# A new order for the products of an attention and MLP-mixer kernel: values in rows

## The chip, the cores and the metric

The kernel runs on one core of one Trainium2 chip. The metric is the device time of one execution in microseconds, as the median of several runs.

## What is computed

For each of 8 x 12 heads, with a sequence of 448 and a head size of 64: scores, a squared ReLU, values. The heads side by side are the 768 channels of an MLP-mixer block.

```python
scores = scale * np.matmul(q, k.transpose(0, 1, 3, 2))
attn = np.maximum(scores, 0.0) ** 2 / S
x = np.matmul(attn, v)                       # then heads side by side
h = np.maximum(xt @ w_tok1, 0.0) @ w_tok2    # xt: tokens and channels swapped
u = x + h.transpose(0, 2, 1)
h2 = np.maximum(u @ w_ch1, 0.0) @ w_ch2
return u + h2
```

Inputs and output are float32; the products run in bfloat16 with sums in float32.

## The kernel before

**Work and names.** The heads are taken four at a time: 24 sets, three to a batch. For set s the operations are, with their names in the program's table:

- `ldk`, `ldq`, `ldv`: loads, by the POOL queue. `T` (L391) transposes k and q on TensorE for sets 0 to 11, and `cp` copies the result to SBUF. From set 12 on, `ik`/`iq` lay k and q out beside each other (L270 or L272) and `xk`/`xq` transpose them by DMA on the SP queue.
- `S{s}.{c}` (L432), c = 0 to 6: the scores of 64 rows of keys for four heads, four matmuls, each on one quarter of the array (64 x 64), into two PSUM banks. `r{s}.{c}.{0,1}` (L264 on ScalarE, L266 on VectorE) are the two evictions with ReLU, one per bank, and `q{s}.{c}` (L439, VectorE) is the square. Ten buffers `sq` hold squares.
- `V{s}.{c}` (L456): the value product of that square, again four matmuls on quarters of the array. The seven of a set add up in the same two banks, and `xe` (L466, L468) evicts them after the seventh.
- `X` (L491) or, from set 8, `xd` (SP queue) transposes for the token mixing; `t1` (L500), `rt`, `t2` (L509), `u` (L513) are its two products, the ReLU and the sum.
- `C1.{b}.{e}` (L545): the first channel product of batch b, twelve blocks of six matmuls on the whole array, evicted by `c1e`. The last two batches take a form with fewer products, `Q` (L617). `P` (L710): the second channel product, seven products of six matmuls for a pair of token tiles, added up by `a`, `b`, `c` and `f` (L725, L727) on VectorE and stored by `st`. `ub` are DMA transposes that bring u to the tokens' layout.
- `fill` (L806): small products without use, which occupy TensorE where the table puts them.

**What sets the order.** Nothing is scheduled at build time: a table, `ORDER`, is a text of some 1950 words, and `Order.run` emits the operations in its order. Each engine executes its own in that order and waits by semaphores for what they need. A word is an operation's name; `:A` or `:D` behind it puts the operation on ScalarE or VectorE, digits name the PSUM banks it writes (eight in all), and `fill:2*7` is seven fill products into bank 2. An operation that writes a bank waits until the operation that read it last is done. The table was written by a search with a model of the engines.

So a score waits for its two banks, that is, for two evictions of an earlier operation; a value waits for its square; an eviction waits for its score and for the buffer `sq`.

Of the kernel before, what the change touches and what calls it, by code (L numbers as in the profile page):

```python
# [61 lines left out]
ldf.1 ldk0.1 ldf.0 ldk0.0 ldk1.1 ldq1.0 cast1.0:A cast1.1:D ldk1.0 ldq1.1 ident cast0.0:A cast0.1:D ldv0.0 T0.1:0  # L62
ldv0.1 T0.0:1 cp0.1:A ldk2.0 cp0.0:D ldq2.1 fill:2*7 S0.0:23 S0.5:45 S0.4:67 ldq2.0 r0.0.0:A r0.0.1:D S0.2:01
r0.5.0:A r0.5.1:D ldk2.1 S0.1:23 r0.2.1:A r0.2.0:D ldv1.1 S0.6:45 r0.1.1:A r0.1.0:D S0.3:10 r0.6.1:A ldv1.0 q0.0:D
r0.6.0:A fill:3*4 T1.0:32 ldq3.1 r0.3.1:A r0.3.0:D ldk3.0 cp1.1:A cp1.0:D ldk3.1 q0.1:D r0.4.1:A fill:5*19 S1.2:54
ldq3.0 S1.3:01 q0.2:D r0.4.0:A S1.4:32 r1.2.0:A ldv2.1 q0.3:D fill:7*3 V0.0:76 r1.2.1:A q0.4:D ldv2.0 r1.3.1:A
S1.0:54 q0.5:D ldk4.0 V0.1 r1.3.0:A V0.2 r1.0.1:D r1.0.0:A wt1.0 T2.0:10 q0.6:D r1.4.1:A V0.3 r1.4.0:A wt1.1 cp2.1:D
V0.4 S1.1:45 cp2.0:A q1.0:D ldk4.1 q1.2:D r1.1.0:A ldq4.0 fill:2*12 S2.1:23 S1.6:01 r1.1.1:A q1.3:D V0.5 ldq4.1
r1.6.1:A V0.6 r1.6.0:D S2.2:45 r2.1.0:A ldv3.0 q1.1:D S1.5:10 xe0.1:A q1.4:D ldv3.1 r1.5.0:A q1.6:D r1.5.1:A wt2
xe0.0:A r2.1.1:D r2.2.0:A q1.5:D ldk5.0 X0.0:2 r2.2.1:A S2.0:61 q2.1:D S2.3:07 xc0.0:A V1.0:34 ldk5.1 r2.0.1:D  # L70
r2.0.0:A V1.1 q2.2:D V1.2 r2.3.0:A ldq5.0 S2.5:52 r2.3.1:A X0.1:1 q2.0:D ldq5.1 T3.0:60 r2.5.0:A xc0.1:D V1.3
r2.5.1:A q2.3:D wc1.1 V1.4 cp3.1:A cp3.0:D S2.6:71 V1.5 r2.6.1:D V1.6 r2.6.0:A S2.4:52 V2.0:60 ldv4.1 q2.5:D xe1.1:A
V2.1 xe1.0:A r2.4.0:D S3.1:17 ldv4.0 r2.4.1:A r3.1.1:D fill:4*4 S3.0:43 ldk6.1 r3.1.0:A X1.1:5 r3.0.1:D V2.2
r3.0.0:A S3.4:27 xc1.1:D t1.0.0:1 r3.4.0:A q2.4:D t1.0.1:3 r3.4.1:A rt0.0:D S3.3:45 rt0.1:A q2.6:D V2.3 r3.3.1:A
V2.4 q3.0:D S3.2:27 r3.3.0:A T4.0:13 q3.1:D r3.2.1:A V2.5 S3.6:54 r3.2.0:A cp4.1:D r3.6.1:A cp4.0:D V3.0:72 V2.6
r3.6.0:A V3.1 q3.2:D ldv5.0 S3.5:34 xe2.1:A t1.1.1:1 r3.5.1:D r3.5.0:A ldq6.0 t2.0.1:5 q3.3:D rt1.1:A X1.0:0 ldv5.1
xe2.0:A V3.2 q3.4:D S4.4:43 xc1.0:A ldk6.0 V3.3 u0.1:D S4.0:16 r4.4.0:A V3.4 X2.0:0 q3.5:D r4.0.1:A X2.1:5 t1.1.0:4
r4.0.0:A xc2.0:D q3.6:D t2.0.0:6 r4.4.1:A ldq6.1 V3.5 rt1.0:A xc2.1:D S4.3:01 u0.0:D V3.6 wc1.0 S4.1:34 r4.3.1:A
t2.1.0:5 r4.3.0:D r4.1.1:A t1.2.0:6 ldq8.0 q4.0:D xe3.0:A t1.2.1:1 xe3.1:A rt2.0:D ldk7.1 t2.1.1:0 u1.0:D r4.1.0:A
t2.2.0:4 ldq8.1 rt2.1:A u1.1:D X3.0:7 ldk7.0 t2.2.1:6 u2.0:D xc3.0:A S4.6:23 q4.1:D ldq7.1 S4.2:51 T5.0:04 u2.1:D  # L80
r4.2.1:A t1.3.0:7 r4.2.0:A ldq9.0 cp5.1:D cp5.0:A r4.6.1:D ldq7.0 C1.0.6:1 q4.2:D rt3.0:A q4.3:D r4.6.0:A V4.0:65
c1e0.6:A S5.0:43 q4.4:D V4.1 S4.5:07 r5.0.1:A r5.0.0:D V4.2 S5.5:21 r4.5.1:A r4.5.0:D C1.0.10:3 r5.5.1:A q5.0:D
r5.5.0:A q4.5:D V4.3 c1e0.10:A S5.1:47 q4.6:D S5.3:01 r5.1.0:A C1.0.11:2 r5.1.1:D r5.3.1:A q5.5:D r5.3.0:A t2.3.0:3
q5.1:D c1e0.11:A C1.0.9:4 ldk8.0 q5.3:D ldv6.0 u3.0:D S5.4:71 c1e0.9:A S5.2:02 ldv6.1 r5.4.1:D C1.0.7:3 r5.4.0:A
r5.2.0:D r5.2.1:A q5.4:D T6.0:41 c1e0.7:A q5.2:D V4.4 V5.0:72 cp6.1:A cp6.0:D S5.6:03 V4.5 V5.1 r5.6.0:D V4.6
r5.6.1:A V5.2 S6.4:41 ldv7.1 xe4.1:D xe4.0:A V5.3 S6.5:03 r6.4.0:A q5.6:D ldk8.1 V5.4 S6.6:65 r6.5.1:A V5.5 r6.5.0:D
# [30 lines left out]
ub2.3 q11.3:D r11.2.1:A C1.2.6:6 r11.2.0:A xe10.1:D xe10.0:A q11.4:D C1.2.2:4 r12.1.0:A xd10 q11.2:D r12.1.1:A
q11.5:D c1e2.6:A P2.1:0 q12.1:D iq14:A st4.0 c1e2.2:D C1.2.0:5 st4.1 ik15:A ldq18.0 f11.1:D ub2.5 iq15:D ldv13.0
V11.0:17 c1e2.0:A S11.6:23 ldv13.1 V11.1 r11.6.0:A r11.6.1:D S12.0:64 st2.1 V11.2 ldk18.1 S12.5:05 r12.0.1:A
r12.0.0:D V11.3 S13.1:23 r12.5.0:A ldq18.1 V11.4 q11.6:D S12.4:46 r12.5.1:A V11.5 ldq16.1 q12.0:D C1.2.4:0 r12.4.1:A  # L120
# [716 lines left out]
```

## Time and profile before

| | |
|---|---|
| median of 3 runs | 351.79 us (350.87 to 352.61) |
| profiled execution | 351.28 us, span 349.5 us |
| instructions | 8983 |
| busy: TensorE / VectorE / ScalarE / GpSimd | 340.4 / 303.4 / 216.5 / 92.2 us |
| mean granted TensorE clock | 0.998 |

In the lines that follow, PE is TensorE, PEld its weight loads, DVE VectorE, ACT ScalarE, POOL GpSimd, and SP the queue of DMAs beside them. A row of a timeline has the start in us from the span's start, the length, the engine, the line, the operation, output and inputs, and how many instructions were merged into it; in brackets stands idle time ahead of it and who ended it. A row by stretches has the busy time of PE, PEld, DVE, ACT and POOL, the granted clock, the share of the DMA engines and GB/s. A matmul's end is modelled, so starts are the safer reading.

### The profile page before, as it was taken

The page shows a single profiled execution, that of the slowest core. Times are in us where ns is not written, and L with a number is a line of the kernel's source. Part 1 is how long each engine was busy: PE and PEld are TensorE (multiplying, and loading weights), DVE is VectorE, ACT ScalarE, POOL GpSimd, SP SyncE. Part 2 cuts the span into 40 slices and gives each one's busy share as a digit, 9 for nine tenths or more (in the row PEclk, how much of TensorE's full clock was granted, in tenths as well). Part 3 has the DMA queues.
Part 4 walks back from the last instruction along what each step waited for, and adds up shares of the span by engine and source line. Part 5 has one row for each costly group of instructions (what it writes and reads, how often), then busy time and mean ns, then how long its engine had stood idle before and what let it go on. Part 6 is the DMA issues. An engine that isn't in the chain of part 4 may idle for free.

```text
span 349.5 us, 8983 instructions
## 1 busy us (share of the span) xinstructions
PE 340.4 (97%) x3598; PEld 190.9 (55%) x3598; DVE 303.4 (87%) x581; ACT 216.5 (62%) x443; POOL 92.2 (26%) x157
## 2 busy tenths in 40 slices
PE   8979999999999999999999999999999999999994
PEld 4546645555555555555555555544556565555662
DVE  2999998889999899988598999899898987678973
ACT  4999887687939099783497927768664411562000
POOL 8884627321461804117304201110200000000000
PEclk9999999999999999999999999999999999999999
DMA  8999997999999999799999925897863524710245
GB/s 152 166 151 183 190 179 106 160 167 112 151 145 182 176 166 190 139 217 172 196 241 134 177 40 94 130 138 153 146 124 86 115 59 89 154 36 0 58 150 156
DMA packets 93434, 48.74 MB, mean 139 GB/s; under 512 B 65808, under 2 KB 90064, under 8 KB 93392
## 3 DMA queue, kind: packets, MB, share of 16 engines
q0 software_dynamic: 25904, 21.47, 44.3%
q1 hardware_dynamic: 67168, 26.30, 42.4%
q8 instruction: 28, 0.46, 0.6%
q10 hardware_dynamic: 320, 0.39, 0.3%
q14 instruction: 14, 0.11, 0.1%
HBM read 43.38 MB, written 11.01 MB: 156 GB/s over the span
## 4 chain that ended last, share of the span: by engine, by line
PE 93%; ACT 4%; DVE 1%; issue 1%; ACTq 0%; DVEq 0%
PE m_ps L710 28%; PE m_ps L545 24%; PE sc_ps L432 9%; PE acc_ps L456 9%; PE m_ps L617 7%; PE t_ps L500 6%; PE h_ps L509 5%; ACT sq L264 3%; PE warm_ps L335 1%; PE kqT_ps L391 1%; PE x_ps L491 1%; DVE sq L439 1%; ACT xT L466 0%; DVE sq L266 0%; ACT kqT L270 0%
## 5 line engine op out<-in xcount | busy, mean ns | idle before, releaser
L264 ACT ACTIVATE sq<-sc_ps 128x448 bf16<-128x448 f32 x222 | 107.9, 572 | 15.3 <-PE sc_ps L432 15.0
L439 DVE TENSOR_TENSOR sq<-sq 128x896 bf16<-128x896 bf16 x168 | 97.0, 614 | 0.0
L545 PE MATMUL m_ps<-uT_sb,wc 128*128 128x448 bf16 x432 | 90.9, 353 | 0.0
L266 DVE TENSOR_SCALAR sq<-sc_ps 128x448 bf16<-128x448 f32 x114 | 66.8, 616 | 12.3 <-PE sc_ps L432 12.2
L264 ACT ACTIVATE r_sb<-m_ps 128x448 bf16<-128x448 f32 (+2 forms) x96 | 42.0, 464 | 45.0 <-PE m_ps L545 43.2
L545 PEld LDWEIGHTS <-wc 128*128 128x128 bf16 x432 | 40.4, 98 | 40.7 <-issue 6.6
L432 PE MATMUL sc_ps<-kqT 64*64 64x448 bf16 x672 | 59.2, 354 | 0.6 <-DVE kqT L272 0.2
L286 POOL DMA_DIRECT2D v_raw<-in_v_dram x48 | 29.3, 620 | 104.7 <-PE acc_ps L456 89.1
L456 PE MATMUL acc_ps<-sq,v_raw 64*64 64x448 bf16 x672 | 56.3, 354 | 0.3
L710 PEld LDWEIGHTS <-r_sb 128*128 128x128 bf16 x336 | 32.5, 98 | 22.9 <-issue 1.3
L286 POOL DMA_DIRECT2D kq_raw<-in_k_dram x48 | 30.2, 640 | 34.3 <-ACT side L270 16.8
L725 DVE TENSOR_TENSOR out_sb<-m_ps,u_sb 128x384 f32<-128x384 f32 x56 | 30.8, 551 | 6.8 <-PE m_ps L710 6.8
L432 PEld LDWEIGHTS <-kqT 64*64 64x64 bf16 x672 | 24.3, 105 | 18.4 <-issue 9.6
L710 PEld LDWEIGHTS <-sums 128*128 128x128 bf16 x252 | 24.5, 98 | 17.0 <-issue 0.4
L286 POOL DMA_DIRECT2D kq_raw<-in_q_dram x46 | 28.4, 628 | 19.8 <-ACT side L270 14.3
L710 PE MATMUL m_ps<-wc_t,r_sb 128*128 128x384 bf16 x168 | 31.2, 326 | 0.0
L710 PE MATMUL m_ps<-wc,r_sb 128*128 128x384 bf16 x168 | 30.6, 326 | 0.0
L513 DVE TENSOR_TENSOR uT_sb<-h_ps,xT 128x448 bf16<-128x448 f32 x48 | 28.6, 613 | 2.2 <-PE h_ps L509 2.2
L710 PE MATMUL m_ps<-wc_t,sums 128*128 128x384 bf16 x168 | 30.1, 326 | 0.0
L456 PEld LDWEIGHTS <-v_raw 64*64 64x64 bf16 x672 | 20.6, 106 | 16.4 <-issue 9.6
L727 DVE TENSOR_TENSOR out_sb<-m_ps,out_sb 128x384 f32<-128x384 f32 x42 | 22.9, 552 | 7.4 <-PE m_ps L710 7.2
L500 PE MATMUL t_ps<-x_sb,wt 128*128 128x256 bf16 (+1 forms) x216 | 25.0, 261 | 0.0
(65 smaller groups left out, 325.2 us busy)
## 6 DMA issues: line engine op xcount, KB each, us to landing
out_dram<-out_sb SPq DMA_DIRECT2D x52, 192.0 KB, 3.1
kq_raw<-in_k_dram POOLq DMA_DIRECT2D x48, 112.0 KB, 5.0
v_raw<-in_v_dram POOLq DMA_DIRECT2D x48, 112.0 KB, 4.6
kq_raw<-in_q_dram POOLq DMA_DIRECT2D x46, 112.0 KB, 5.0
wc<-in_moe_w_ch_dram POOLq DMA_DIRECT2D x2, 1152.0 KB, 10.7
wc<-in_moe_w_ch_dram POOLq DMA_DIRECT2D x3, 576.0 KB, 9.2
u_sb<-uT_sb SPq DMA_TRANSPOSE x54, 3.4
sums<-in_moe_w_ch_dram POOLq DMA_DIRECT2D x1, 576.0 KB, 10.8
```

The source lines that it names most:

```text
L264: nc.scalar.activation(out, ps, AF.Relu)
L266: nc.vector.tensor_scalar(out=out, in0=ps, scalar1=0.0, scalar2=None, op0=ALU.max)
L286: nc.gpsimd.dma_start(out=raws[t][s % NR[t]][64 * half:64 * (half + 1)], in_=src[b, h0:h0 + 2].rearrange('e (p c) d -> p e (c d)', c=KC))
L432: nc.tensor.matmul(o.ps[e][64 * half:64 * (half + 1), :S], lhsT=lhsT, rhs=rhs, start=True, stop=True, skip_group_check=True)
L439: sq_ops[s, c] = [add(Op(f'q{s}.{c}', 'DVE', lambda o: nc.vector.tensor_tensor(out=buf, in0=buf, in1=buf, op=ALU.mult), ev))]
L456: nc.tensor.matmul(o.ps[half][64 * e:64 * (e + 1), :S], lhsT=r[rows, e, c * D:(c + 1) * D], rhs=sq[rows, e, :], start=c == 0, stop=c == KC ...
L500: nc.tensor.matmul(o.ps[:, j, :], lhsT=wt1[:, c, j * 128:(j + 1) * 128], rhs=x_sb[:, p0:p1, c, :], start=c == 0, stop=c == 3)
L513: nc.vector.tensor_tensor(out=uTs[bb % 2][:, 2 * i + a, off:off + S].rearrange('n (c p) -> n c p', c=KC), in0=t2.ps[:, :S].rearrange('n (p ...
L545: nc.tensor.matmul(ps[:, :S], lhsT=wc1[:, g, e * 128:(e + 1) * 128], rhs=uT[:, g, off:off + S], start=g == 0, stop=g == CC - 1)
L617: nc.tensor.matmul(banks[into][:, :S], lhsT=lhs[:, g, k * 128:(k + 1) * 128], rhs=rhs[:, g], start=after is None and g == 0, stop=g == GH ...
L710: nc.tensor.matmul(banks[into][:, :HN], lhsT=lhs[:, e], rhs=wc2[w][:, e], start=after is None and e == 0, stop=e == EH - 1, skip_group_che ...
L725: nc.vector.tensor_tensor(out=out_[:, cols].rearrange('n (g d) -> n g d', d=128), in0=banks[into][:, :HN].rearrange('n (g d) -> n g d', d= ...
```

## The change

Only the text of `ORDER` differs. Operations, loads, buffers and the code that emits them are the same. The new text comes from a new search with a model in which a value product that follows another value product of its set does not wait for it. Almost every line of the table is new; four of the lines around the value products of set 10 show its kind:

```diff
-c1e2.3:A q10.2:D q11.0:D V10.0:71 xd9 c1e2.8:A S11.1:64 V10.1 r11.1.0:A r11.1.1:D S11.4:32 V10.2 S11.3:05 r11.4.1:A
-r11.4.0:D V10.3 ub2.1 S11.5:64 r11.3.1:A V10.4 r11.3.0:D S12.1:23 r11.5.0:A V10.5 q11.1:D S11.2:50 r11.5.1:A V10.6
+f12.1:D P4.2 f21.1:D ub2.2 P3.2 f21.2:D ub2.5 S11.3:20 f12.2:D S11.1:47 V10.0:63 V10.1 r11.1.0:A r11.1.1:D V10.2
+S11.5:51 st5.1 r11.3.1:A r11.3.0:D V10.3 V10.4 r11.5.0:A S11.4:47 ub2.3 q11.1:D V10.5 r11.5.1:A V10.6 S12.1:02
```

The counts of the whole table:

| | before | after |
|---|---|---|
| values that directly follow a value of their set on TensorE | 9 | 77 |
| rows of 2 / 3 / 4 values of a set | 7 / 1 / 0 | 30 / 13 / 7 |
| stretches of quarter-array products (T, S, V) between whole-array ones | 59 | 56 |
| of these after C1.0.6, the first channel product | 45 | 41 |
| fill products, in groups | 49 in 6 | 52 in 4 |
| score evictions on ScalarE / VectorE | 222 / 114 | 237 / 99 |
| all operations that can go on either, ScalarE / VectorE | 420 / 574 | 429 / 565 |

The last row counts every operation that bears an `:A` or `:D`.

**TensorE at the value products of set 10.** The names are `v_raw1` for the values' weights, `sq` for the squares, `kqT2` for the keys and queries of set 11, and `acc_ps` and `sc_ps` for the banks of values and scores. Before, the end of V10.5 and the start of S11.2:

```order
L456 LDWEIGHTS v_raw1_80
L456 MATMUL acc_ps_2710<-sq_87,v_raw1_80 64x448
L432 LDWEIGHTS kqT2_84
L432 MATMUL sc_ps_2777<-kqT2_84 64x448 [waits Activation_49]
L432 LDWEIGHTS kqT2_84
L432 MATMUL sc_ps_2778<-kqT2_84 64x448 [waits DVE_49]
```

Now, the end of V10.3 and the start of V10.4:

```order
L456 MATMUL acc_ps_2732<-sq_87,v_raw1_80 64x448
L456 LDWEIGHTS v_raw1_80
L456 MATMUL acc_ps_2732<-sq_87,v_raw1_80 64x448
L456 LDWEIGHTS v_raw1_80
L456 MATMUL acc_ps_2731<-sq_87,v_raw1_80 64x448
```

Where a score stood behind each value, with a wait for an eviction on ScalarE in its first matmul and one on VectorE in its second, a second value of the set stands behind the first, and it waits for no engine here.

**VectorE at the same place.** These are the evictions of scores of sets 11 and 12 (L266), squares (L439) and the eviction of the values (L468). Before:

```order
L266 TENSOR_SCALAR sq<-sc_ps 128x448 x3
L439 TENSOR_TENSOR sq<-sq 128x896 x2
L468 TENSOR_SCALAR xT_65<-acc_ps 128x448
L439 TENSOR_TENSOR sq<-sq 128x896 x4
L266 TENSOR_SCALAR r_sb<-m_ps 128x384
```

Now:

```order
L266 TENSOR_SCALAR sq<-sc_ps 128x448 x2
L439 TENSOR_TENSOR sq<-sq 128x896
L266 TENSOR_SCALAR sq<-sc_ps 128x448
L439 TENSOR_TENSOR sq<-sq 128x896 x2
L266 TENSOR_SCALAR sq<-sc_ps 128x448
```

Three score evictions in one row have become two, one and one with squares between them, and the eviction of the values has gone to ScalarE.

**ScalarE at the start.** The rows are the copies of the transposed keys and queries of sets 0, 1 and 2 (`kqT`) and the score evictions between them. Before:

```order
L270 ACTIVATE kqT_82<-kqT_ps 128x896
L264 ACTIVATE sq<-sc_ps 128x448 x7
L270 ACTIVATE kqT_83<-kqT_ps 128x896
L264 ACTIVATE sq<-sc_ps 128x448 x9
L270 ACTIVATE kqT_84<-kqT_ps 128x896
L264 ACTIVATE sq<-sc_ps 128x448 x4
```

Now:

```order
L270 ACTIVATE kqT_82<-kqT_ps 128x896
L264 ACTIVATE sq<-sc_ps 128x448 x8
L270 ACTIVATE kqT_83<-kqT_ps 128x896
L264 ACTIVATE sq<-sc_ps 128x448 x8
L270 ACTIVATE kqT_84<-kqT_ps 128x896
L264 ACTIVATE sq<-sc_ps 128x448 x5
```

One eviction has moved ahead of the copy for set 1, and one more stands behind the copy for set 2.

More of the change, by code (lines that the diff above doesn't have):

```diff
@@ L61 @@
 ORDER = """
[L62 to L86, printed above, removed]
@@ L117 @@
[L117 to L120, printed above, removed]
-q12.5:D r12.4.0:A r13.1.0:A r13.1.1:D V11.6 c1e2.4:A S12.3:56 q12.4:D t1.9.0:4 xe11.0:A r12.3.1:D r12.3.0:A xe11.1:D
@@ L197 @@
-st27.0.0 f12.12:D st24.1 f12.13:D st24.0 st26.1.384 st26.0.384
+ldf.1 ldk0.1 ldf.0 ldk0.0 ldk1.1 ldq1.1 ldq1.0 cast1.0:A cast1.1:D ldk1.0 ident cast0.0:D cast0.1:A ldv0.0 T0.1:0
+ldv0.1 T0.0:1 cp0.1:A ldq2.1 cp0.0:D ldk2.1 fill:2*7 S0.2:23 S0.6:45 S0.5:67 r0.2.0:D r0.2.1:A ldk2.0 S0.3:01
+r0.5.0:A r0.5.1:D S0.1:32 ldq2.0 r0.6.1:A r0.6.0:D S0.0:67 r0.1.1:A ldv1.1 r0.1.0:D r0.0.0:A S0.4:54 ldv1.0 r0.0.1:A
+r0.3.1:D fill:2*4 T1.0:23 ldk3.0 r0.3.0:A q0.1:D r0.4.1:A ldq3.1 q0.0:D cp1.1:A cp1.0:D ldk3.1 r0.4.0:A q0.2:D
@@ new lines @@
+ldq3.0 fill:6*26 S1.2:67 S1.4:10 S1.3:43 q0.3:D r1.2.0:A S1.1:25 ldv2.0 r1.2.1:A q0.4:D ldv2.1 r1.1.0:A V0.0:67
+q0.5:D V0.1 r1.1.1:A ldk5.1 r1.3.1:D r1.3.0:A T2.0:25 wt1.1 q0.6:D r1.4.1:A V0.2 r1.4.0:A V0.3 cp2.1:D wt1.0 S1.6:34
+cp2.0:A q1.2:D ldq4.1 q1.3:D r1.6.1:A fill:0*15 S2.3:01 ldq4.0 S1.5:52 r1.6.0:A q1.1:D V0.4 V0.5 r1.5.0:A ldk4.0
+V0.6 q1.4:D S1.0:43 r1.5.1:A ldk4.1 r1.0.1:D r1.0.0:A S2.2:52 q1.6:D xe0.1:A wt2 xe0.0:A q1.0:D ldv3.0 r2.2.0:A
+q1.5:D V1.0:34 r2.2.1:A S2.1:76 ldv3.1 V1.1 r2.3.0:D r2.3.1:A V1.2 V1.3 ldk6.1 q2.2:D S2.5:52 r2.1.0:A V1.4 S2.0:01
@@ new lines @@
+t2.7.0:6 t2.7.1:7 u6.1:D ldq14.1 P2.0:2 u7.1:D ldv10.1 f12.0:D t1.8.0:3 f11.0:D u7.0:D st0.0 S9.5:54 rt8.0:A
+S10.1:17 V9.0:02 r9.5.1:D xk12 V9.1 r9.5.0:A V9.2 r10.1.1:D S10.5:63 r10.1.0:A V9.3 V9.4 r10.5.0:A q9.5:D S10.3:45
+t2.8.0:7 st0.1 r10.5.1:A q10.1:D C1.1.6:1 r10.3.1:A xq12 r10.3.0:D iq13:A u8.0:D V9.5 c1e1.6:A V9.6 q10.3:D st1.0
+S10.4:63 T11.0:54 ldv12.1 xe9.1:A xe9.0:D st1.1 r10.4.1:A S10.6:71 s1.1:D ldk15.0 t2.8.1:2 cp11.0:A P2.2:0 r10.6.1:D
+ldq17.0 r10.6.0:A s2.1:D ldq15.1 cp11.1:A P1.1:3 s1.2:D ldq16.0 s3.1:D r10.4.0:A s2.2:D S11.0:15 ldk15.1 ik14:A
@@ new lines @@
+st14.0 q22.1:D r23.2.0:A st15.0 t2.20.0:2 q23.0:D c1e5.8:A ub5.0 C1.5.0:5 u19.1:D q23.2:D V22.0:14 u20.0:D c1e5.0:A
+S23.3:73 V22.1 V22.2 r23.3.0:A r23.3.1:D V22.3 V23.0:06 S23.6:25 st13.0 q23.3:D V23.1 S23.5:73 r23.6.1:A V22.4 ub6.1
+r23.6.0:D V23.2 r23.5.1:A V23.3 V22.5 r23.5.0:A V22.6 q23.6:D S23.4:52 xe22.1:A C1.5.3:3 xe22.0:D st15.1 r23.4.1:A
+r23.4.0:D xd22 q23.5:D C1.5.9:7 c1e5.3:A q23.4:D t2.20.1:4 c1e5.9:A y3.0:D t1.21.0:1 u20.1:D V23.4 y3.1:D rt21.0:A
+V23.5 V23.6 P1.8:2 s1.9:D xe23.1:A s1.8:D xe23.0:A P5.9:5 s2.9:D xd23 a.8:D s2.8:D P1.9:3 s3.8:D s3.9:D P6.8 a.9:D
@@ L198 @@
+st27.0.384 P2.12:2 f21.13:D st27.1.384 P3.12 st26.0.0 f11.12:D st27.0.0 P3.13 st27.1.0 f12.12:D st24.1 f12.13:D
+st24.0 st26.0.384 st26.1.384
 """
```

216 lines of the change are left out of this document (113 added, 103 removed).

## The prediction

> **What bounds the kernel now.** I read the busy shares first, then the chain of work, then the engines by stretch of time, and last the timeline of single instructions.
>
> ```profile
> PE 340.4 (97%) x3598; PEld 190.9 (55%) x3598; DVE 303.4 (87%) x581; ACT 216.5 (62%) x443; POOL 92.2 (26%) x157
> ...
> PE 93%; ACT 4%; DVE 1%; issue 1%; ACTq 0%; DVEq 0%
> ```
> ```profile
> 8.00:42.00 34.00, 31.01 (x672) 19.75 (x673) 33.38 (x65) 32.54 (x70) 24.03 (x40) 1.00 1.13 171
> 42.00:150.00 108.00, 108.00 (x1315) 59.30 (x1314) 101.05 (x190) 79.97 (x162) 38.14 (x63) 1.00 1.08 157
> 150.00:262.00 112.00, 112.00 (x998) 61.43 (x996) 99.81 (x191) 77.76 (x163) 23.19 (x39) 1.00 0.99 150
> 262.00:345.00 83.00, 82.86 (x544) 47.40 (x542) 66.48 (x131) 22.92 (x45) 0.00 (x0) 1.00 0.38 88
> ```
>
> TensorE is busy for 97% of the span, carries 93% of the chain, and the granted clock is 1.00 in all four stretches. From 8 to 42 us it is another engine that sets the pace: VectorE works 33.38 of 34 us and ScalarE 32.54, while TensorE has 31.01, fill products among them. After 42 us TensorE looks full. But a matmul's record there runs from its start to a modelled end of about 0.36 us, so records overlap and hide short waits. A wait is seen only in the distance between starts, so I read those.
>
> ```profile
> 126.51 0.51 PE L432 MATMUL sc_ps<-kqT 64*64 64x448 bf16 x4
> 126.70 0.51 PE L456 MATMUL acc_ps<-sq,v_raw 64*64 64x448 bf16 x4
> 126.89 0.67 PE L432 MATMUL sc_ps<-kqT 64*64 64x448 bf16 x4
> 127.19 0.56 PE L456 MATMUL acc_ps<-sq,v_raw 64*64 64x448 bf16 x4
> 127.68 2.44 PE L545 MATMUL m_ps<-uT_sb,wc 128*128 128x448 bf16 x12
> 129.96 1.14 PE L710 MATMUL m_ps<-wc,r_sb 128*128 128x384 bf16 x6
> 130.93 1.30 PE L545 MATMUL m_ps<-uT_sb,wc 128*128 128x448 bf16 x6
> 132.16 0.38 PE L456 MATMUL acc_ps<-sq,v_raw 64*64 64x448 bf16 x4
> 132.38 0.36 PE L432 MATMUL sc_ps<-kqT 64*64 64x448 bf16 x4
> 132.56 0.36 PE L456 MATMUL acc_ps<-sq,v_raw 64*64 64x448 bf16 x4
> ...
> 134.08 0.51 PE L456 MATMUL acc_ps<-sq,v_raw 64*64 64x448 bf16 x4
> 134.52 0.74 PE L545 MATMUL m_ps<-uT_sb,wc 128*128 128x448 bf16 x3
> ```
>
> Three prices stand in these rows. A channel matmul takes 2.28 / 12 = 0.19 us (127.68 to 129.96). A score or a value, four matmuls on quarters of the array, also takes 0.19 (132.38 to 132.56). Passing from whole-array matmuls to quarter ones costs extra: six channel matmuls from 130.93 should end at 132.07, and the value starts at 132.16, so 0.09; its follower comes 0.22 later in place of 0.19, so 0.03 more. The way back costs the same 0.09. A stretch of quarter-array work thus costs about **0.21 us** beside its work.
>
> The fourth price is a wait. From 126.89 to 127.19 and from there to 127.68 are 0.30 and 0.49, where 0.19 and 0.19 + 0.09 were due: 0.11 + 0.21 us. From 134.08 to 134.52 it is 0.16. VectorE shows why in the first case:
>
> ```profile
> 125.44 1.69 DVE L266 TENSOR_SCALAR sq<-sc_ps 128x448 bf16<-128x448 f32 x3 [0.39 <-PE sc_ps L432]
> 127.04 1.15 DVE L439 TENSOR_TENSOR sq<-sq 128x896 bf16<-128x896 bf16 x2
> ```
>
> Three score evictions stand on VectorE and end at 127.13. The score S11.2, in the row at 126.89, writes the bank that the third of them frees, and its other half cannot start before. So where scores and values alternate, a score comes every 0.38 us and leaves one eviction to VectorE, which needs 0.54 for each (1.69 less a last latency of 0.61, halved). The banks run out near the end of a long stretch. I find such waits of 0.06 to 0.21 us in ten stretches after 46 us, 1.9 us in all; here are the first and the last of the ten:
>
> ```profile
> 107.77 0.48 PE L432 MATMUL sc_ps<-kqT 64*64 64x448 bf16 x4
> 108.18 0.55 PE L509 MATMUL h_ps<-wt,r_sb 128*128 128x448 bf16 x2
> ```
> ```profile
> 224.67 0.93 PE L456 MATMUL acc_ps<-sq,v_raw 64*64 64x448 bf16 x16
> 225.42 0.48 PE L432 MATMUL sc_ps<-kqT 64*64 64x448 bf16 x4
> 225.84 0.83 PE L500 MATMUL t_ps<-x_sb,wt 128*128 128x256 bf16 x6
> ```
>
> In both, 0.41 to 0.42 lie between starts where 0.28 was due.
>
> **The change, part by part.** *Values in a row.* Value products that follow a value of the same set: 9 before, 77 now. Do they cost more than 0.19?
>
> ```profile
> 21.69 0.74 PE L456 MATMUL acc_ps<-sq,v_raw 64*64 64x448 bf16 x12
> 22.25 0.44 PE L432 MATMUL sc_ps<-kqT 64*64 64x448 bf16 x4
> ...
> 24.20 0.57 PE L456 MATMUL acc_ps<-sq,v_raw 64*64 64x448 bf16 x8
> 24.58 0.38 PE L432 MATMUL sc_ps<-kqT 64*64 64x448 bf16 x4
> ```
>
> Three values of set 1 in a row take 0.56 and two take 0.38: 0.19 each. No stall of its own, so the 68 added followers cost **0**.
>
> A rule speaks against this. The Trainium skill, "TensorE: Matmul & The Clock Gate", section "Part 3: Packing small matmuls", says that a weight load overlaps running matmuls only where its row group differs. Two values use the same row groups, so by it each follower would wait for its load, and the sum would be worse by the second rival's price below. The rows just quoted disagree: 0.19 with no gap.
>
> *Stretches.* After the first channel product (C1.0.6) the table of before has 45 stretches of quarter-array work, the new one 41. 4 x 0.21 = **-0.84 us**, all on the chain, since TensorE is full there.
>
> *Waits for banks.* Now the pattern is score, value, value, or more values: a score each 0.57 us, enough for VectorE's 0.54. I laid each table's TensorE row end to end at the prices above and took, for each bank, the work between its last user and its next. Among the scores after C1.0.6, 58 of 262 bank uses had under 1.1 us before and 15 have now; among all kinds of product, 12 had under 0.9 and none has. An eviction is 0.54 to 0.61 us and two handovers, so 0.9 is about the least that does without a wait. The ten stretches' 1.9 us should nearly go. The ends are 0 (evictions queue as before) and -1.9; I take **-1.4**, nearer to the second, since the tight uses fell by three quarters.
>
> *Start.* Fill groups change from six (49 products) to four (52), and early stretches from 14 to 15. They fall where TensorE waits anyway, so they are covered by the evictions; if that cover were gone, three fills and one stretch would be under 0.4 us. What counts is how much ScalarE and VectorE do before C1.0.6, which starts at 41.62.
>
> ```profile
> 41.62 1.30 PE L545 MATMUL m_ps<-uT_sb,wc 128*128 128x448 bf16 x6
> ```
> ```profile
> 12.47 4.13 ACT L264 ACTIVATE sq<-sc_ps 128x448 bf16<-128x448 f32 x9
> ```
> ```profile
> L270 ACT ACTIVATE kqT<-kqT_ps 128x896 bf16<-128x896 bf16 x12 | 11.2, 948 | 0.6 <-PE kqT_ps L391 0.3
> ```
>
> ScalarE gets 76 instructions ahead of it in place of 73, VectorE 68 in place of 67. Those on ScalarE are three more evictions at 0.45 (4.13 less 0.57, over 8) and a copy of 0.95 for a shorter one: at most +1.9 us. VectorE's one is at most +0.54. Against that TensorE has three more scores done by then, 0.57 us. Ends: 0 - 0.57 = -0.6 and 1.9 - 0.57 = +1.3. VectorE is the fuller engine in the row of 8 to 42 us (33.38 against 32.54), so I stay near its price: 0.54 - 0.57, rounded to **+0.1** because ScalarE's first copy for set 1 now stands behind eight evictions in place of seven.
>
> *Queues.* The loads and transposes are issued in a new order. By the same laying-out, the shortest TensorE work between the release of a used buffer and the next use of it is 8.6 us for loads in both tables, and for the transposes of the SP queue 9.2 us before and 9.1 now; the page gives 5.0 us from issue to landing for most loads:
>
> ```profile
> kq_raw<-in_k_dram POOLq DMA_DIRECT2D x48, 112.0 KB, 5.0
> ...
> x_sb<-xT SPq DMA_TRANSPOSE x16, 4.6
> ```
>
> So 0. From P2.10 on the products keep their order, and so does the end: 0.
>
> **Sum:** -0.84 - 1.4 + 0.1 = -2.1 us. The profiled execution took 351.28 us (span 349.5 and 1.8 around it), so 349.2; from the median of the runs, 351.79, it would be 349.7. I say **349.4**. A half per cent, 1.8 us, is about what a measurement of this kernel can tell from no change, and -2.1 lies just beyond it.
>
> **Rivals.** *The waits stay.* VectorE has 101.05 of 108 us of work until 150; its queue, not the banks' spacing, may set the evictions, and new tight places may open. Then only the stretches pay, and the start may take its upper end: -0.84 to +0.5, 350.4 to 351.8. For it speaks VectorE's load; against it, that the new table gives VectorE 15 score evictions fewer (99 for 114).
>
> *Followers wait after all.* If a value waited for its weight load:
>
> ```profile
> L456 PEld LDWEIGHTS <-v_raw 64*64 64x64 bf16 x672 | 20.6, 106 | 16.4 <-issue 9.6
> ```
>
> 68 x 0.106 = +7.2, so 356.4 with the gains kept. The rows at 21.69 and 24.20 speak against it.
>
> *Slower: rows of values outrun their squares.* A value needs its square, which VectorE makes in 0.54 while TensorE uses one in 0.19. If the squares of a row are only being made when the row begins, a row of n waits (n - 1) x 0.35. The new table has 13 rows of three and 7 of four (before: one of three), at most 13 x 0.70 + 7 x 1.05 = 16.5 us. It decides at the point where the last square of a row isn't finished when its first value starts. If this held for one row in three, +5.5, so 354.7. For it: VectorE's 33.38 of 34 us at the start. Against it: TensorE work between a score and its value. After C1.0.6, ten values had under 3 us before, now two (V23.3 with 1.7, V7.5 with 2.4).
>
> **How the numbers follow.** Forecast (waits mostly go): 0.48, with its own range 348.3 to 350.2, from -3 to -1. The waits stay: 0.32. Values outrun squares: 0.17. Followers wait: 0.03. The range leaves out 2 in 10, so it reaches from 347.6 (all 1.9 us and the start's lower end: -0.84 - 1.9 - 0.6 = -3.3, and 0.4 for the spread of runs) to 353.1 (one row in six outruns its squares: -2.1 + 2.7, with the start's upper end 1.2 more). The bound for faster lies at 350.0, so the forecast's case holds faster by over 0.5%: 0.48. Waits that stay give a time within 0.5%: 0.32. The last two cases give slower: 0.20.
>
> **What would show it.** In the changed trace, values in a row start 0.19 apart; long stretches end on 0.28, not 0.41, before the next whole-array matmul; C1.0.6 starts within 1.3 us of 41.62. The last matmul of TensorE, now near 344.9, shows the whole gain. I am wrong if distances inside rows of values are over 0.3, if VectorE's evictions still end just as the scores' second halves start, or if the clock falls below 1.00 in any stretch.

## The result, and the profile after

| | before | after |
|---|---|---|
| median of 20 runs each | 351.63 us (350.58 to 353.14) | 350.32 us (348.93 to 351.89) |
| ratio | | 0.9962 [0.9945, 0.9978] |
| profiled execution (span) | 351.28 us (349.5) | 351.30 us (349.5) |
| mean granted clock of the profiled execution | 0.998 | 0.995 |

The new table is faster by 0.4%, 1.3 us, where 2.1 to 2.4 us were forecast. In the two profiled executions nothing is gained at all, and that makes them worth reading: two changes of 3 us stand in them, one against the other. Ratios, here and below, leave out the few executions that took some 5 to 10 us more than the others of their kernel, among them two of the ten of a kernel spliced from both tables.

The page's busy times and the chain by engine say only that little has changed:

```profile
PE 339.4 (97%) x3601; PEld 188.9 (54%) x3601; DVE 300.5 (86%) x573; ACT 221.0 (63%) x451; POOL 92.2 (26%) x157
...
PE 94%; DVE 2%; DMA 1%; issue 1%; ACT 1%; POOL 0%; POOLq 0%
```

The busy times by stretch of time point to the start. The granted clock is the third number from the end:

```profile
8.00:42.00 34.00, 30.17 (x612) 18.24 (x612) 31.91 (x62) 31.70 (x68) 21.34 (x35) 0.95 1.16 176
42.00:150.00 108.00, 108.00 (x1372) 59.60 (x1365) 100.47 (x190) 83.19 (x167) 42.58 (x70) 1.00 1.15 157
150.00:262.00 112.00, 112.00 (x1007) 60.70 (x1005) 96.78 (x183) 78.75 (x168) 21.36 (x36) 1.00 0.94 146
262.00:345.00 83.00, 82.85 (x549) 47.27 (x546) 69.09 (x134) 24.09 (x47) 0.00 (x0) 1.00 0.42 92
```

From 8 to 42 us all three engines do less than before and the clock is 0.95 in place of 1.00. Two landmarks on TensorE, C1.0.6 and the last products, split the execution:

```profile
44.63 3.58 PE L545 MATMUL m_ps<-uT_sb,wc 128*128 128x448 bf16 x18
...
342.74 2.11 PE L710 MATMUL m_ps<-wc,sums 128*128 128x384 bf16 x12
```

C1.0.6 starts at 44.63, 3.0 us later than before's 41.62. The last products start at 342.74, which is exactly where they started before. So everything from C1.0.6 on became 3.0 us shorter: from its start to the start of the last matmul it was 302.91 us and is 299.90.

**The gain.** A stretch of quarter-array work at the place where the prediction read its wait:

```profile
126.55 0.36 PE L432 MATMUL sc_ps<-kqT 64*64 64x448 bf16 x4
126.73 0.55 PE L456 MATMUL acc_ps<-sq,v_raw 64*64 64x448 bf16 x8
127.11 0.36 PE L432 MATMUL sc_ps<-kqT 64*64 64x448 bf16 x4
127.30 0.55 PE L456 MATMUL acc_ps<-sq,v_raw 64*64 64x448 bf16 x8
127.68 0.36 PE L432 MATMUL sc_ps<-kqT 64*64 64x448 bf16 x4
127.97 1.31 PE L545 MATMUL m_ps<-uT_sb,wc 128*128 128x448 bf16 x6
```

Two values in a row take 0.38, and the last score is followed by the whole-array product after 0.29. The 0.30 and 0.49 of before are gone. The same holds at two stretches near the places of the first and the last of the ten:

```profile
106.76 0.36 PE L432 MATMUL sc_ps<-kqT 64*64 64x448 bf16 x4
107.06 0.55 PE L509 MATMUL h_ps<-wt,r_sb 128*128 128x448 bf16 x2
```
```profile
223.35 0.93 PE L456 MATMUL acc_ps<-sq,v_raw 64*64 64x448 bf16 x16
224.10 0.55 PE L432 MATMUL sc_ps<-kqT 64*64 64x448 bf16 x8
224.59 3.58 PE L545 MATMUL m_ps<-uT_sb,wc 128*128 128x448 bf16 x18
```

0.30 lie between the starts of the last score and what follows, where 0.41 lay before (in the second, two scores and the way back take 0.49, so 0.30 for the last); and four values in a row take 0.75.

**The loss.** TensorE at the start, with idle times in brackets, and the clock just behind:

```profile
19.00 1.10 PE L432 MATMUL sc_ps<-kqT 64*64 64x448 bf16 x8
21.29 0.38 PE L456 MATMUL acc_ps<-sq,v_raw 64*64 64x448 bf16 x4 [1.19 <-DVE sq L439]
...
22.61 0.98 PE L432 MATMUL sc_ps<-kqT 64*64 64x448 bf16 x8
23.46 0.90 PE L391 MATMUL kqT_ps<-ident,kq_raw 64*64 64x64 bf16 x56
24.17 0.38 PE L432 MATMUL sc_ps<-kqT 64*64 64x448 bf16 x4
26.13 0.59 PE L432 MATMUL sc_ps<-kqT 64*64 64x448 bf16 x4 [1.58 <-DVE kqT L272]
```
```profile
26.00:28.00 2.00, 1.87 (x21) 0.94 (x24) 1.68 (x4) 1.53 (x4) 0.00 (x0) 0.50 1.01 123
28.00:30.00 2.00, 2.00 (x24) 0.76 (x16) 1.16 (x2) 1.41 (x4) 0.00 (x0) 0.66 1.09 185
```

TensorE waits for the square of V1.0 and then for the copy of set 3's keys and queries (S3.3, at 26.13). From 26 to 28 us the granted clock is 0.50, and VectorE and ScalarE, which set the pace here, run out of work as well: 1.16 and 1.41 of 2 us in the second row. In finer stretches the clock is 1.00 up to 25.96 us, 0.50 from 25.97 to 29.37, and 1.00 again from 29.38. Half the clock for 3.4 us takes 1.7 / 349.5 = 0.005 off the mean of an execution, so a mean of 0.995 or less points to a fall while TensorE had work. A mean of 0.996 does not: one execution below (the old table with fills) has it from a clock of 0.50 behind its last product alone.

Not every run loses its clock. In 13 of the 20 runs of the new table the mean is 0.996 or more, and their median span is 347.6 us; in the other 7 it is 0.992 to 0.995, and theirs is 349.2. The kernel before loses its clock as well: on the three chips of the experiments in 18 of 65 executions, with a median of 351.78 us against 351.14 for the other 47. So the new table changed less how often the clock falls than what a fall goes with: 1.5 us in place of 0.6. Where it doesn't fall, 351.14 has become 349.44.

The clock is not all that differs between executions: without a fall, the spans of the new table still reach from 347.1 to 350.1 us. Part of such a spread are pauses of TensorE inside one operation for which the profile names no cause: 0.72 us at 34.09 in the run with rotation and fills below, 0.51 at 35.48 in the run with free turns. What makes them is open.

### The profile page after: what moved, and what is told of

The parts are those of the page before. It is cut to its first block, busy times and chain, and to the rows that moved or that the text cites. A ratio compares the mean times of both kernels' runs of the same rounds, so it can differ in the third digit from the quotient of the medians.

```text
span 349.5 us, 8996 instructions
## 1 busy us (share of the span) xinstructions
PE 339.4 (97%) x3601; PEld 188.9 (54%) x3601; DVE 300.5 (86%) x573; ACT 221.0 (63%) x451; POOL 92.2 (26%) x157
## 4 chain that ended last, share of the span: by engine, by line
PE 94%; DVE 2%; DMA 1%; issue 1%; ACT 1%; POOL 0%; POOLq 0%
PE m_ps L710 28%; PE m_ps L545 24%; PE sc_ps L432 10%; PE acc_ps L456 10%; PE m_ps L617 7%; PE t_ps L500 6%; PE h_ps L509 6%; PE kqT_ps L391 2%; DMA kq_raw<-in_k_dram 1%; PE x_ps L491 1%; PE fill_ps L806 1%; DVE sq L439 1%; DVE sq L266 1%; ACT sq L264 1%; DVE kqT L272 0%
## 5 line engine op out<-in xcount | busy, mean ns | idle before, releaser
L264 ACT ACTIVATE sq<-sc_ps 128x448 bf16<-128x448 f32 x237 | 114.6, 569 | 15.5 <-PE sc_ps L432 14.3
L439 DVE TENSOR_TENSOR sq<-sq 128x896 bf16<-128x896 bf16 x168 | 97.5, 616 | 0.6
L545 PE MATMUL m_ps<-uT_sb,wc 128*128 128x448 bf16 x432 | 89.8, 353 | 0.0
L266 DVE TENSOR_SCALAR sq<-sc_ps 128x448 bf16<-128x448 f32 x99 | 58.0, 617 | 6.6 <-PE sc_ps L432 4.1
L264 ACT ACTIVATE r_sb<-m_ps 128x448 bf16<-128x448 f32 (+3 forms) x88 | 38.8, 470 | 29.2 <-PE m_ps L545 26.6
L432 PE MATMUL sc_ps<-kqT 64*64 64x448 bf16 x672 | 54.7, 356 | 2.2 <-DVE kqT L272 1.8
L456 PE MATMUL acc_ps<-sq,v_raw 64*64 64x448 bf16 x672 | 48.2, 359 | 1.3 <-DVE sq L439 1.2
L264 ACT ACTIVATE r_sb<-t_ps 128x512 bf16<-128x512 f32 (+1 forms) x22 | 13.3, 604 | 27.5 <-PE t_ps L500 27.3
L432 PEld LDWEIGHTS <-kqT 64*64 64x64 bf16 x672 | 19.4, 106 | 20.7 <-issue 11.1
L456 PEld LDWEIGHTS <-v_raw 64*64 64x64 bf16 x672 | 19.8, 108 | 16.6 <-issue 8.0
```

Of the source, the lines that this page charges most:

```text
L264: nc.scalar.activation(out, ps, AF.Relu)
L266: nc.vector.tensor_scalar(out=out, in0=ps, scalar1=0.0, scalar2=None, op0=ALU.max)
L432: nc.tensor.matmul(o.ps[e][64 * half:64 * (half + 1), :S], lhsT=lhsT, rhs=rhs, start=True, stop=True, skip_group_check=True)
L439: sq_ops[s, c] = [add(Op(f'q{s}.{c}', 'DVE', lambda o: nc.vector.tensor_tensor(out=buf, in0=buf, in1=buf, op=ALU.mult), ev))]
L456: nc.tensor.matmul(o.ps[half][64 * e:64 * (e + 1), :S], lhsT=r[rows, e, c * D:(c + 1) * D], rhs=sq[rows, e, :], start=c == 0, stop=c == KC ...
L545: nc.tensor.matmul(ps[:, :S], lhsT=wc1[:, g, e * 128:(e + 1) * 128], rhs=uT[:, g, off:off + S], start=g == 0, stop=g == CC - 1)
```

## The experiments

The theory after the result: the gain from C1.0.6 on is the spacing of the scores (waits) and the fewer stretches, and the start takes part of it back by two waits and the clock. The rivals: the gain comes from VectorE's lighter load; rows of values are worth something by themselves; the start is set by ScalarE and VectorE whatever TensorE does. All ratios are against the kernel before on the same chip.

**Halves of the table, put together.** Two kernels take one table up to C1.0.6 and the other behind it. The first has the start of before:

```diff
 t1.3.0:7 r4.2.0:A ldq9.0 cp5.1:D cp5.0:A r4.6.1:D ldq7.0
-C1.0.6:1 q4.2:D rt3.0:A q4.3:D r4.6.0:A V4.0:65
+ldk8.0 rt3.0:A S4.5:17 r4.5.1:A r4.5.0:A ldk9.1 ldv6.1 S5.0:64 q4.2:D S5.2:37 r4.6.0:A C1.0.6:2 q4.3:D
```

> The table of before up to the first channel product (C1.0.6), the new table from there on; the ten operations that only the new start had done by then follow first (three scores among them). Theory: the new table gains from C1.0.6 on (302.91 us from there to the last matmul before, 299.90 after, in the profiled executions) and loses at the start (C1.0.6 at 41.62 and 44.62 us). Then this kernel has both good halves: before less 2.2 to 2.9 us, ratio to before 0.992 to 0.994, C1.0.6 at about 42.4. Rival: the new table gains evenly and the late C1.0.6 is only work done ahead; then 0.996, as the whole new table.

Measured: 352.48 us, ratio 1.0018 [0.9996, 1.0040], a miss. The timeline shows why. Ahead of C1.0.6 stand three scores with no other work between them:

```profile
43.51 0.57 PE L427 MATMUL sc_ps<-kqT 64*64 64x448 bf16 x8 [0.70 <-ACT r_sb L259]
44.53 0.38 PE L427 MATMUL sc_ps<-kqT 64*64 64x448 bf16 x3 [0.44 <-ACT sq L259]
45.40 5.22 PE L540 MATMUL m_ps<-uT_sb,wc 128*128 128x448 bf16 x18 [0.49 <-ACT sq L259]
```

(Its lines lie five lower.) TensorE waits 0.70, 0.44 and 0.49 us for evictions on ScalarE, ahead of the scores and behind them. The splice itself made these waits. The clock fell as well, twice: from 22 to 30 us it was 0.82, and from 45.39 to 48.80 it was 0.50, so that the 18 channel matmuls of the last row take 5.22 us where 18 x 0.19 = 3.4 were due; the mean is 0.987 to 0.992 in six of twelve runs. So this kernel doesn't tell what it was made to tell.

The second has the new start and before's order behind it:

> The new table up to C1.0.6, the table of before from there on. Theory of a bad start and a good rest: slower than before by 1 to 2.5 us, ratio 1.003 to 1.007, with the waits at the ends of long stretches back (scores 0.4 us before the next whole-array matmul). Rival of an even gain: 1.000 or below.

Measured: 353.94 us, ratio 1.0062 [1.0041, 1.0083], as expected. Behind the same start the new order of the rest is worth 1.0062 - 0.9962 = 1.0%, some 3.5 us, which agrees with the 3.0 of the traces within the intervals. No timeline of this kernel is read.

The first splice was then mended: the three scores stand behind the first three channel products, one each.

```diff
 ldk8.0 C1.0.6:5 q4.2:D rt3.0:A r4.6.0:A S4.5:17 q4.3:D r4.5.1:A ldk9.1 r4.5.0:A ldv6.1 C1.0.10:2
 c1e0.6:A q4.4:D S5.0:64 ldk8.1 r5.0.1:A q4.5:D r5.0.0:A q4.6:D C1.0.11:0 c1e0.10:A S5.2:37
```

> The table of before up to C1.0.6 and the new one behind it, as in the first such run, but the three scores that the new table has ahead of C1.0.6 now stand one behind each of the first three channel products, where those products cover the wait for their banks. Theory (the first splice lost its time to these three scores waiting for evictions): from C1.0.6 to the last matmul 299.9 plus 0.57 for the three scores and 0.42 for two more stretches, and C1.0.6 itself at before's 34.96 us behind T0.0: 349.2 to 350.0, ratio 0.993 to 0.996. Rival (the new order pays only behind its own start, since it counts on squares and evictions being ahead): over 351, ratio 0.998 or more.

Measured: 350.70 us, ratio 0.9974 [0.9955, 0.9992], between the two. From C1.0.6 on it takes 302.05 us, 1.15 more than expected. In the distances between starts I find 1.34 us of waits at seven places where the new table has 0.21 at two, which is that difference; the largest is just behind the splice:

```profile
46.63 0.36 PE L456 MATMUL acc_ps<-sq,v_raw 64*64 64x448 bf16 x4
47.25 0.38 PE L432 MATMUL sc_ps<-kqT 64*64 64x448 bf16 x4 [0.26 <-ACT sq L264]
```

C1.0.6 itself comes 35.61 us behind T0.0 where 34.96 was expected, behind a clock of 0.50 from 21.28 to 24.68 us: 0.65 more, about what a fall goes with in the kernel before. 5 of its 12 runs have a mean of 0.995 or less. So the new order keeps a part of its worth behind another start. That it loses the rest to queues which are not where it counts on them is shown at the row above; 0.3 of the 1.34 us stand inside a run of transposes, without a cause in the profile, and another 0.3 in a wait for a square at 270 us.

**Order or engines.** The new table has 15 score evictions fewer on VectorE. One kernel gives the evictions from set 5 on the engines of before, another gives before's table those of the new one; 99 words differ in each, such as

```diff
-r5.0.0:A r5.2.0:A r5.2.1:D r5.3.0:D r5.5.0:D r5.4.1:A
+r5.0.0:D r5.2.0:D r5.2.1:A r5.3.0:A r5.5.0:A r5.4.1:D
```

> The new table, but the evictions of scores of sets 5 and later on the engines that the table of before gives them (224 on ScalarE and 112 on VectorE in all, for 237 and 99). Theory (the spacing of the scores on TensorE removes the waits for banks): from C1.0.6 to the last matmul at most 300.4 us (299.9 in the new table, 302.9 before), median 350.0 to 350.8, ratio 0.995 to 0.998. Rival (VectorE's lighter load removes them): at least half of the 1.7 us of waits comes back, 300.8 or more, median 351.2 or more, ratio 0.999 or more.

> The other half: the table of before with the evictions of scores of sets 5 and later on the engines that the new table gives them (235 on ScalarE and 101 on VectorE). Theory: the ten ends of long stretches keep at least 1.4 of their 1.9 us, 302.4 to 303.2 from C1.0.6 to the last matmul, ratio 0.999 to 1.002. Rival: the waits fall to 0.9 or less, 301.9 or less, ratio 0.997 or less.

Measured: 353.93 us, 1.0073 [1.0049, 1.0097], and 354.55 us, 1.0089 [1.0066, 1.0112]. From C1.0.6 on 304.38 and 306.10 us, with 4.85 us of waits in 25 places and 5.06 in 26. Both are slower than either whole table, and both theories fall in the size: neither the order nor the share of the engines removes the waits alone, and the runs do not separate the two, since each brings waits of its own. VectorE's list of waits after 46 us names what is new, first with the new order and then with the old one:

```profile
DVE sq L439 <- ACT sq L264: 3.2, 8, 0.9
```
```profile
DVE sq L439 <- ACT sq L264: 2.7, 7, 0.8
```

Squares on VectorE wait for ScalarE's half of the same score, 8 and 7 times; in the lists of before and of after there is no such row. The largest wait of the first kernel, on TensorE and on VectorE:

```profile
94.09 0.68 PE L432 MATMUL sc_ps<-kqT 64*64 64x448 bf16 x8
95.59 1.14 PE L710 MATMUL m_ps<-wc,r_sb 128*128 128x384 bf16 x6 [0.82 <-DVE sq L266]
```
```profile
93.72 0.62 DVE L468 TENSOR_SCALAR xT<-acc_ps 128x448 bf16<-128x448 f32 x1
94.25 0.75 DVE L329 TENSOR_TENSOR wc_t<-wc,wc_t 128x1152 bf16<-128x1152 bf16 x1
94.92 0.62 DVE L266 TENSOR_SCALAR sq<-sc_ps 128x448 bf16<-128x448 f32 x1
```

The eviction that P1.0 waits for now stands on VectorE, behind an eviction of values and an operation on weights (`wc_t`) that P1.0 could do without at that time. In the new table VectorE has no score eviction there, and ScalarE makes eight in one row:

```profile
92.63 3.60 ACT L264 ACTIVATE sq<-sc_ps 128x448 bf16<-128x448 f32 x8
```
The engine of an eviction, its place among the squares and the order of TensorE are one decision.

**Rows or turns.** In the new table the values and scores of 22 stretches behind C1.0.6 are put in turn again, on TensorE alone:

```diff
-V12.0:43 V12.1 V12.2 V12.3 S13.4:25 V12.4 V12.5 V12.6 S13.3:07 S13.6:16 C1.2.7:2
+V12.0:43 S13.4:25 V12.1 S13.3:07 V12.2 S13.6:16 V12.3 V12.4 V12.5 V12.6 C1.2.7:2
```

> The new table with values and scores in turn again, as far as a stretch has both: 22 stretches after C1.0.6 are re-sorted on TensorE alone, 46 followers in place of 77, the other engines' order and the counts as they are. Theory of the evictions' pace: scores 0.38 us apart outrun VectorE, and waits of 0.1 to 0.3 us return at the stretches' ends, 1 to 2.5 us in all: ratio to before 0.999 to 1.003. Rival: the spacing of the scores does not matter, only VectorE's lighter load and the fewer stretches do: 0.996.

Measured: 356.83 us, ratio 1.0138 [1.0116, 1.0161]. The direction was right, the size far off: 6.0 us of waits in 31 places, where before's table has 1.9. This stretch of the new table, on TensorE and ScalarE:

```profile
144.35 0.57 PE L432 MATMUL sc_ps<-kqT 64*64 64x448 bf16 x8
...
145.70 0.74 PE L456 MATMUL acc_ps<-sq,v_raw 64*64 64x448 bf16 x12
146.27 0.55 PE L432 MATMUL sc_ps<-kqT 64*64 64x448 bf16 x8
146.75 1.31 PE L545 MATMUL m_ps<-uT_sb,wc 128*128 128x448 bf16 x6
```
```profile
145.08 3.21 ACT L264 ACTIVATE sq<-sc_ps 128x448 bf16<-128x448 f32 x7
```

and in turn (its lines, too, lie five lower):

```profile
145.76 0.44 PE L451 MATMUL acc_ps<-sq,v_raw 64*64 64x448 bf16 x4
146.87 0.43 PE L427 MATMUL sc_ps<-kqT 64*64 64x448 bf16 x4 [0.67 <-ACT sq L259]
147.05 1.00 PE L451 MATMUL acc_ps<-sq,v_raw 64*64 64x448 bf16 x16
147.98 1.31 PE L540 MATMUL m_ps<-uT_sb,wc 128*128 128x448 bf16 x6
```
```profile
144.97 0.54 ACT L259 ACTIVATE sq<-sc_ps 128x448 bf16<-128x448 f32 x1
146.27 2.73 ACT L259 ACTIVATE sq<-sc_ps 128x448 bf16<-128x448 f32 x6 [0.75 <-PE acc_ps L451]
```

The same twelve operations take 2.40 us in rows (144.35 to 146.75) and 3.68 in turn (144.30 to 147.98). ScalarE shows a cause that the prediction did not have: it sits idle for 0.75 us with a score to evict, until a value product has ended. An eviction writes a buffer `sq`, of which there are ten, and a value frees one. Values that come later free buffers later, so evictions start later, banks come free later, and the next score waits (0.67 us here, for ScalarE). This kernel's list of waits has 2.5 us of them on ScalarE, and the new table's has none of this kind there:

```profile
ACT sq L259 <- PE acc_ps L451: 2.5, 5, 0.8
```

So this kernel doesn't price a turn by itself. The next one does: 25 scores move one place ahead, into the last gap of a row, only where their banks have been free for long.

```diff
-V10.5 r11.5.1:A V10.6 S12.1:02
+V10.5 r11.5.1:A S12.1:02 V10.6
```

> The new table with 25 scores moved one place ahead, in between the last two values of a row, only where TensorE has over 1.1 us of work between the last user of the score's banks and its new place; 60 values follow a value of their set in place of 77. Theory (a row of values is worth nothing by itself, it only spaces the scores; where banks are free long before, the turn does not matter): from C1.0.6 to the last matmul 299.7 to 300.3, median 350.0 to 350.7, ratio 0.995 to 0.998. Rival (a score between two values of a set costs something of its own; 46 turns everywhere cost 6.5 us, so 25 some 3.5, or 17 fewer followers some 1.5): 301.4 to 303.4, median 351.8 to 353.8, ratio 1.000 to 1.007.

Measured: 349.80 us, ratio 0.9949 [0.9931, 0.9968]. By the time the theory holds: a row is worth nothing by itself, as far as 25 places tell. The profiled execution has 301.3 us from C1.0.6 on, more than the theory's 300.3, but it was one of the longer two of nine (span 349.9, median 348.0). Of its 1.63 us of waits 0.14 stand at one of the 25 places, behind V22.6. The large ones lie elsewhere: 0.69 inside the transposes ahead of S7.1, again a pause without a cause in the profile (at 67.89), and 0.6 among the last products `P`, which in part wait for VectorE's sums.

**The start.** Four kernels change the start of the new table, and one that of before. The first adds two groups of fill products:

```diff
-V1.0:34
+fill:3*10 V1.0:34
...
-S3.3:76
+fill:7*16 S3.3:76
```

> The new table with 26 more fill products in the two waits of TensorE before 27 us: ten ahead of V1.0, sixteen ahead of S3.3. Nothing else moves. Theory of the clock: TensorE's two waits there let the granted clock fall to 0.50 at 26 to 28 us, where five values take 0.37 us each for 0.19; with the fills the clock stays at 1.00 and the time falls by 0.8 to 1.5 us against the new table, ratio to before 0.992 to 0.994. Rival: the waits themselves cost, not the clock; then the time is the new table's, 0.996, or a little above for the fills' 0.2 us.

Measured: 349.50 us, 0.9948 [0.9929, 0.9966]; in the profiled execution the clock is 1.00 from 8 to 60 us, and none of 11 runs has a mean of 0.995 or less. The direction is the one expected; the ratio misses the 0.992 to 0.994 that the theory gave.

Next, no fills, but the scores 0, 2 and 6 of set 1 rotated, so that V1.0's square is made first:

```diff
-S1.2:67 S1.4:10 S1.3:43 S1.1:25 S1.6:34 S1.5:52 S1.0:43
+S1.0:67 S1.4:10 S1.3:43 S1.1:25 S1.2:34 S1.5:52 S1.6:43
```

> The new table with the scores 0, 2 and 6 of set 1 in rotated places, so that the square of V1.0 is made first and not last; nothing else is touched. In the new table TensorE waits 1.82 us ahead of V1.0 for that square. Theory (the start's loss is this wait, the next one of 1.77 us ahead of S3.3, and the granted clock of 0.50 and 0.66 that follows them in some runs): V1.0 starts up to 1.0 us earlier, two long waits no longer stand so close together, the clock stays at 1.00 from 26 to 30 us, and the median is 349.0 to 349.8, ratio 0.993 to 0.995. Rival (ScalarE and VectorE set the pace of the start, so TensorE only waits elsewhere): V1.0 starts earlier, but the wait ahead of S3.3 grows by as much, C1.0.6 is no earlier, and the clock falls as often as before: 350.0 to 350.6, ratio 0.996 to 0.997.

Measured: 350.31 us, 0.9966 [0.9941, 0.9991]: the rival's time. V1.0 starts 1.4 us earlier behind T0.0 (13.09 us, 14.51 in the new table), S3.3 only 0.4 (18.96, 19.34), and six of twelve runs have a mean clock of 0.995 or less.

```profile
23.53 0.38 PE L432 MATMUL sc_ps<-kqT 64*64 64x448 bf16 x4
25.45 0.38 PE L432 MATMUL sc_ps<-kqT 64*64 64x448 bf16 x4 [1.54 <-DVE kqT L272]
```
```profile
22.00:30.00 8.00, 6.29 (x143) 3.31 (x139) 8.00 (x17) 7.96 (x18) 4.31 (x8) 1.00 1.18 181
```

VectorE is busy for 8.00 of 8 us and ScalarE for 7.96. S3.3 waits for a copy that stands in a full queue, so an earlier V1.0 only moves TensorE's wait: from V1.0 to the last score ahead of S3.3 are 3.96 us here (19.57 to 23.53) and 2.88 in the new table. The rotation with fills ahead of both places (6 and 16):

> The same rotation, with 6 fill products ahead of V1.0 and 16 ahead of S3.3. If only the clock is left to save, the fills hold it at 1.00 and the median is that of the runs of the new table at full clock, 349.4, or up to 0.5 less for the earlier V1.0: 348.9 to 349.5, ratio 0.992 to 0.994. If the fills delay more than they save: 349.5 to 350.3.

Measured: 349.31 us, 0.9933 [0.9907, 0.9959]. This is the fastest of all kernels by its median, but no different from the fills alone within what the runs can tell. And the one group ahead of S3.3 alone, with V1.0's wait left as it is:

> The new table with 16 fill products ahead of S3.3 only, so that the wait of 1.8 us ahead of V1.0 stays and the one ahead of S3.3 is filled but for some 0.5. Theory (it takes both waits, in one window of some 8 us, to bring the clock down): the clock stays at 0.996 or more in all but one or two runs, median 349.3 to 349.8, ratio 0.993 to 0.996. Rival (one wait of 1.8 us is enough, as the rotated table suggests, where only the one ahead of S3.3 was left and six of twelve runs had 0.992 to 0.995): three or more of ten runs below 0.996, median 349.9 to 350.6, ratio 0.996 to 0.998.

Measured: 349.51 us, 0.9947 [0.9926, 0.9967]; none of seven runs is below 0.997. With one group of fills at one wait the clock holds:

```profile
20.84 0.38 PE L456 MATMUL acc_ps<-sq,v_raw 64*64 64x448 bf16 x4 [1.19 <-DVE sq L439]
...
24.15 1.05 PE L806 MATMUL fill_ps<-out_sb 128*128 128x128 bf16 x16
25.68 0.38 PE L432 MATMUL sc_ps<-kqT 64*64 64x448 bf16 x4 [0.47 <-DVE kqT L272]
...
42.72 2.44 PE L545 MATMUL m_ps<-uT_sb,wc 128*128 128x448 bf16 x12
```

From S3.3 to C1.0.6 are 17.04 us here and 18.50 in the profiled execution of the new table: the fall of the clock cost 1.46 us. The fills themselves have no part in this: the run with values and scores in turn has the start of the new table without fills, its clock held, and it takes 17.04 as well. That this kernel's clock held does not show that both waits are needed: in the rotated table the wait ahead of V1.0 was down to 0.7, and the clock still fell in half of the runs. The wait ahead of S3.3 is the one that decides. Over the three kernels with fills there, none of 25 runs has a mean clock of 0.995 or less, against 7 of 20 of the new table and 6 of 12 of the rotated one. Their ratios of 0.9933 to 0.9948 lie below the new table's 0.9962, but the intervals overlap. The kernel with free turns has the same start without fills and 0.9949, with a fall in one of its nine runs. So that the fills hold the clock is shown, and how much of the median it is worth is known to some 0.5 us at best.

Last, before's table with 16 fills ahead of X0.0, where its TensorE waits 1.9 us. In the profile of before:

```profile
20.96 0.40 PE L491 MATMUL x_ps<-ident,xT 128*128 128x128 bf16 x4 [1.71 <-ACT xT L466]
```

> The table of before with 16 fill products ahead of X0.0, where its TensorE waits 1.9 us. Theory (the table of before loses its clock in only a quarter of its runs, and then 0.5 us): the median stays within 0.3 us of before, ratio 0.999 to 1.001, so that the gain of the new table with fills is not owed to fills alone. Rival (fills help any start): 350.6 or less, ratio 0.997 or less.

Measured: 351.58 us, 1.0002 [0.9985, 1.0018], as the theory says. Here, too, the clock holds: none of 12 runs has a mean of 0.995 or less. Yet they are no faster than the runs of before on the same chip without a fall (median 350.97). So holding the clock is not by itself a gain; where these runs lose what it should bring, 0.6 us, is open.

## Why the prediction was partly right

- **Values in a row, 0:** right. Two take 0.38 and four 0.75, so 0.19 each. The rule of the Trainium skill that was weighed ("TensorE: Matmul & The Clock Gate", "Part 3: Packing small matmuls") would have made it 356.4; no follower waits for its load here.
- **Stretches, -0.84:** right. 90 changes between quarter- and whole-array work after C1.0.6 have become 82; at the 0.093 us that the trace of before gives for one, -0.74.
- **Waits for banks, -1.4:** right, and a little low. Distances after C1.0.6 that exceed their price by over 0.05 us fall from 13 places with 1.88 us to 2 with 0.21: -1.67. With the three scores that now stand ahead of C1.0.6, -0.57, the sum is -2.98 where -3.01 was measured and -2.81 stood in the prediction. That VectorE's pace of a score each 0.57 us was the cause is only part of it: the runs with exchanged engines show that the order of squares has to fit, and the run with turns that the buffers `sq` have to be freed.
- **Start, +0.1:** wrong, and this is the step that failed. The prediction put C1.0.6 0.67 us later and counted three fills and one stretch as covered. Without a fall of the clock it is 1.16 us later in the run with one group of fills (36.12 behind T0.0 for 34.96) and 1.36 in the run with turns, which has none; less 0.57 for the scores this is +0.6 to +0.8, inside the bounds of -0.6 to +1.3. In the profiled execution it is 2.88 later, +2.3, of which 1.46 are the clock. In the medians it comes to -1.3 + 3.0 = 1.7 later, +1.1 or so. The prediction counted the work of ScalarE and VectorE and not where TensorE would idle. It said that a clock below 1.00 in any stretch would show it wrong, and had no price for it. It went by one profile of before, with 1.00 in all four stretches, while the clock of before falls in over a quarter of its executions.
- **The outcome:** of its cases, the waits did go, which was the forecast's; but its time of 348.3 to 350.2 was missed by 0.1, and faster by over 0.5%, the outcome with 0.48, did not come. The time lies just short of the 350.4 to 351.8 given to the case in which waits stay, and its outcome, a time within 0.5%, came by another cause. That the runs without a fall, 347.6 us and 1.8 around the span, give the 349.4 of the forecast to the tenth is in part luck: the waits brought 0.3 us more than their term, and the start took at least 0.5 more than its own. The slower rivals found no place: no row of values outran its squares.

## What to carry to other kernels

Where an engine looks full, lay its operations end to end at their own prices and compare the distances between starts; 1.7 us of waits that no idle figure showed went here, and 1.4 of them had been predicted that way. An order, the engines of the evictions and the buffers' release belong together, and taking half of a searched table can be worse than either whole. Look at a new order's longest waits on TensorE also for what they do to the clock behind them; a few fill products in the right wait held the clock here, worth 1.5 us in an execution that would have lost it, and in a similar wait of the old table they held it and were worth nothing. And read the granted clock by stretches before two profiles are compared: here, two with the same time hid a gain of 3 us.

## What was not expected of the hardware

A wait of TensorE of 1.96 us from start to start (24.17 to 26.13) was followed by a granted clock of 0.50 for 3.4 us (25.97 to 29.37). It happened in some runs only: the mean was 0.995 or less in 7 of 20. The Trainium skill, "TensorE: Matmul & The Clock Gate", section "What's actually happening", tells of activity windows of about 3.4 us that run freely, and of half the clock after an idle one. The 3.4 us at half, and that it came in some runs and not in others, agree with that. That the window has to be idle does not: in the 3.41 us ahead of the fall, 22.55 to 25.96, TensorE was busy for 1.88 us, so a window that was 45% idle was followed by half the clock. It isn't always: the profiled execution of the run with turns has the same wait of 1.96 us (24.26 to 26.22), and its mean clock is 1.000. Where the line lies, these traces do not show.
